# Value pieces and idle matmuls laid out anew between the last head and the first expert, and the second expert's digits computed ahead of its comparisons

## The chip, the cores and the metric

The kernel runs on one core of one Trainium2 chip. The metric is the device time of one execution in microseconds; the comparison uses the median of several executions. A profiled execution gives a trace besides, and its span (first to last instruction) is a little shorter than the time.

## The reference, cut to what matters

```python
def reference(q, k, v, proj, moe_w_gate, moe_w1, moe_w2):
    # attention: 4 batches x 8 heads, 768 positions, 64 wide; a query sees the keys of its own hash bucket
    mask = q_bucket[:, :, :, None] == k_bucket[:, :, None, :]          # buckets: 6 sign bits of q@proj, k@proj
    scores = np.where(mask, scale * q @ k.T, -1e9)
    x = softmax(scores) @ v                                           # -> 3072 tokens x 512
    # mixture of 8 experts, each takes exactly 3072/8 = 384 tokens
    logits = x @ w_gate                                               # 3072 x 8
    for idx in np.argsort(-logits.flatten()):                         # greedy: best (token, expert) pair first
        tok, e = idx // 8, idx % 8
        if assigned[tok] >= 0 or counts[e] >= cap: continue
        assigned[tok] = e; counts[e] += 1
    for e in range(8):
        out[assigned == e] = relu(x[assigned == e] @ w1[e]) @ w2[e]
```

## The kernel before

The 32 heads run one after the other. A head has six key blocks of 128; for each, TensorE makes scores, ScalarE the exponentials, GpSimd or VectorE their low halves, and TensorE multiplies with the values. The last two heads are treated apart: their gate logits come first, so that the assignment of tokens to experts can begin, and their product with the values is cut into **value pieces**, a list `s.rest` of 76 closures (`mains`): per piece three matmuls of 64 columns (L363 to L365), and after each 18 pieces a `close` of three matmuls (L370 or L371) whose result ScalarE scales into X, which SyncE stores. Six are taken up earlier; 70 are left.

The greedy assignment is done in eight phases, one for each expert that fills up (`Moe.phase`). A phase finds a threshold digit by digit: six digits of the logits' bits, and for each a **round** on the path VectorE, TensorE, VectorE, TensorE: VectorE compares the tokens' digits with all values of the digit (L630, `zcmp`), TensorE counts per expert (L640 and 24 matmuls of L641 in the program before, eight columns each), VectorE finds which values reach the expert's room (L743, `zsat`, `zhit`), TensorE sums that into the digit found (L751), VectorE subtracts it (L759, `zd`) and compares the next digit. After the sixth digit come L769 and L770, a chain of small VectorE operations up to the running sum `zcum` (L796), two matmuls (L799, L800), the chain to the one-hot rows `ohp` of the members (L812), 24 matmuls that collect the members' numbers (L815), and `zidx`, with which GpSimd gathers 384 rows of x (L884). Expert weights are fetched as soon as the expert's number is known (L892).

Phase 0 stands between attention and the first expert, and nothing else than value pieces can run in TensorE's pauses. The list `FL` says how many pieces `more(i)` takes at the i-th place: `more(0)` before the last eight counts of the first round, `more(2*l+1)` behind the counts of round l, `more(2*l+2)` behind its L751. Where no pieces are left, **idle matmuls** fill the pauses (`warm`, L682: constants times constants into a tile that nobody reads), so many at each place as `KW` says, of 128 columns unless a third argument says otherwise. Then x is transposed in three chunks (L948), split into halves by ScalarE and VectorE (L949, L950), and the first expert's first layer begins (L965).

Phase 1, for the second expert, runs during the first expert's work: the table `EP` says at which step of it each part of the phase is issued. Its digits 1 to 5 (`digit`, L625 on VectorE) are issued behind its first comparisons and counts. All order on an engine is the order in which the code is written (`manual_schedule`).

Of the kernel before, what the change touches and what calls it, by code (L numbers as in the profile page):

```python
# [14 lines left out]
ALU = mybir.AluOpType  # L15
# [489 lines left out]
E1=[8, 12, 16, 19, 21, 24, 26, 29, 31, 34, 36, 43, 44, 51]  # L505
H1=[2, 0, 2, 2, 0, 3, 0, 2, 2, 0, 1, 0, 0, 0]
ES=[-16, -13, -11, -8, -2, 1, 5, 8, 12, 15, 19, 21, 29, 38]
EP={1: [8, 12, 16, 18, 21, 24, 26, 29, 32, 35, 38, 40, 44, 51], 2: [-5, -3, 1, 4, 8, 11, 15, 18, 22, 25, 29, 32, 39, 47], 3: [-8, -5, -2, 1, 4, 6, 10, 13, 17, 20, 26, 29, 36, 45], 4: [-10, -8, -5, -2, 2, 5, 8, 11, 15, 18, 22, 26, 34, 42]}
WL=[4, 46]
W1=[[], [57, 62, 69, 74], [53, 64, 66, 72], [50, 57, 62, 67], [46, 52, 59, 63], [44, 52, 58, 63]]  # L510
HP={2: [0, 0, 3, 1, 2, 0, 2, 2, 1, 3, 0, 0, 0, 0], 3: [0, 0, 0, 2, 2, 2, 2, 3, 2, 3, 0, 0, 0, 0], 4: [0, 0, 2, 2, 2, 0, 2, 2, 2, 2, 0, 0, 0, 0]}
# [3 lines left out]
OWN=[(2, 0, 0), (3, 0, 0), (4, 0, 0), (5, 0, 0), (3, 1, 3), (4, 1, 3), (5, 1, 3)]  # L515
XS=[56, 56, 57, 57]
XD=[0, 9, 7, 4]
KW=[1,0,5,7,[0,0,6],15,5,1]
SC=[16, 16, 36]
FL=[21, 3, 6, 3, 6, 3, 6, 3, 6, 3, 6, 3, 99]  # L520
XSC=8.0
WSC=64.0
class Moe:
# [72 lines left out]
    def t(s,shape,dt,name,**k): return s.sp.tile(shape,dt,name=name,**k)  # L596
# [79 lines left out]
    def more(s,i):  # L676

        n=FL[i] if i<len(FL) else 0
        while n and s.rest: s.rest.pop(0)(); n-=1
# [4 lines left out]
    def phase(s,ph):  # L684

        nc,NC=s.nc,s.NC; V=nc.vector; T=nc.tensor; G_=nc.gpsimd
# [3 lines left out]
        def ps(): return s.ps0() if first and s.ps0 else s.ps()  # L690
# [3 lines left out]
        if not last:  # L694
            P=s.Z
            D,E,mxu=P["D"],P["E"],P["mxu"]; d=E[:,0]
            CMP=[P["cmp"][l and 1+l%2] for l in range(6)]
            if not first:
                for i,f in enumerate(s.best(P,0,NC)):
                    if ph==1 and i==4: yield  # L700
                    f()
                s.gate=P["OH"][0:1,0,0:1]
                for c0,c1_ in ((0,12),(12,NC)) if ph==1 else ((0,NC),):
                    if ph==1: yield
                    s.compare(CMP[0],0,d,c0,c1_)
                if ph==1: s.gate=CMP[0][0:1,NC//2-1,0,0:1]
            tot=0
            for l,w in enumerate(WID):
                tot+=w; u=2.0**-tot; cmp=CMP[l]
                yield  # L710
                pc=ps()
                if l==0 or first:
                    for c0,c1_ in blocks if first else ((0,NC),):
                        if l: s.compare(cmp,l,d,c0,c1_)
                        if first and l==0 and c1_==NC: s.more(0)
                        s.count(pc,P,cmp,l,c0,c1_)
                    if first:
                        s.more(2*l+1)
                        if not s.rest:
                            if wp is None: wp=s.wps()  # L720
                            s.warm(KW[0],wp)
                        if l==0: s.digit(P,1,slice(0,NC))
                        if l<5:
                            dE=t([128,NC],F32,"dE"); V.scalar_tensor_tensor(dE,D[:,l+1],2.0**-sum(WID[:l+2]),d,op0=ALU.mult,op1=ALU.add)
                    else:
                        for q in range(1,6): s.digit(P,q,slice(0,NC))
                        V.tensor_tensor(E[:,1],D[:,1],s.sc[:,1],op=ALU.mult)
                        for q in range(2,6): nc.scalar.activation(E[:,q],D[:,q],AF.Copy,scale=2.0**-sum(WID[:q+1]))
                        if ph>2:
                            for _ in range(2): s.fill()  # L730
                else:
                    nt=s.count4(pc,P,cmp)

                def carry():
                    g=ps()[:,0:NC]
                    T.matmul(g,s.identb,d,start=True,stop=False)
                    T.matmul(g,s.identb,E[:,l+1],start=False,stop=False)
                    return g
                if not first and 0<l<5: g=carry()
                if l==5: break  # L740
                sat=t([128,8],BF,"sat"); hit=t([128,1],BF,"hit") if l==0 or first else s.hits[l%2]; J=NT[l]
                if l==0 or first:
                    V.tensor_scalar(sat[0:J],pc[0:J,0:8],0.0,0.0,op0=ALU.is_ge,op1=ALU.max,accum_out=hit[0:J])  # L743
                    if first and l<4: s.digit(P,l+2,slice(0,NC))
                else:
                    V.tensor_tensor(sat[0:32],pc[96:128,24:32],nt,op=ALU.is_ge)
                    V.reduce_max(hit[0:32],sat[0:32],axis=AX.X)
                if not first: yield
                if first:
                    pn=ps(); n=pn[:,0:1]  # L750
                    T.matmul(n,s.us[l][0:J],hit[0:J],start=True,stop=True); s.more(2*l+2)  # L751
                    if wp is not None: s.warm(KW[1],wp)
                else:
                    if l==0: g=carry()
                    T.matmul(g,s.nus[l],hit.to_broadcast([128,NC]),start=False,stop=True)
                if l==0 and ph==2:
                    s.fill(); s.fill()
                d2=t([128,NC],BF,"d2",bufs=6)
                if first: V.tensor_tensor(d2,dE,n.to_broadcast([128,NC]),op=ALU.subtract)  # L759
                else:  # L760
                    s.compare(CMP[l+1],l+1,g); V.tensor_copy(d2,g); s.gate=CMP[l+1][0:1,NC//2-1,0,0:1]
                d=d2

            sat=s.satl; s.gate=sat[0:1,0:1]; nn=t([128,1],F32,"nn"); nf=t([128,1],F32,"nf")
            if first: V.tensor_scalar(sat[0:32],pc[0:32,0:8],0.0,None,op0=ALU.is_ge)
            else: V.tensor_tensor(sat[0:32],pc[96:128,24:32],nt,op=ALU.is_ge)
            if not first: yield
            pe=ps()
            T.matmul(pe[:,0:8],s.ones,s.wtb,start=True,stop=False)  # L769
            T.matmul(pe[:,0:8],s.tiny,sat,start=False,stop=True)  # L770
            if first:
                s.more(12)
                if wp is None: wp=s.wps()
                s.warm(KW[2],wp,256)
            V.reduce_max(nn,pe[:,0:8],axis=AX.X)
            wg=t([128,NC],F32,"wg"); e0=t([128,NC],F32,"e0"); A1=t([128,8,NC],BF,"A1"); cc=t([128,8],BF,"cc")
            V.tensor_scalar(nf,nn,ROUND*2.0**-32,ROUND*2.0**-32,op0=ALU.add,op1=ALU.subtract)
            V.scalar_tensor_tensor(wg,d,nn,mxu,op0=ALU.is_gt,op1=ALU.mult)
            V.tensor_scalar(cm,nn,nf,2.0**32,op0=ALU.subtract,op1=ALU.mult)
            if not first: V.tensor_tensor(s.asg,s.asg,wg,op=ALU.add)  # L780
            V.scalar_tensor_tensor(e0,d,nf,mxu,op0=ALU.is_equal,op1=ALU.mult)
            if first: s.widx(ph,cm,t)
            for k,a in enumerate((wg if first else s.asg,e0)): V.tensor_tensor(STb[:,k*NC:k*NC+NC],a,cm.to_broadcast([128,NC]),op=ALU.is_equal)
            if not first: s.widx(ph,cm,t)
        else:
            s8=t([128,8],F32,"s8"); e0=t([128,NC],F32,"e0")
            V.tensor_scalar(c1,s.rem,4.0e4,None,op0=ALU.is_lt)
            V.tensor_tensor(s8,c1,s.wt,op=ALU.mult)
            V.reduce_max(cm,s8,axis=AX.X)
            s.widx(ph,cm,t)  # L790
            V.tensor_scalar(e0,s.asg,cm,None,op0=ALU.is_equal)
            V.tensor_tensor(STb[:,0:NC],e0,s.un,op=ALU.add)
            V.memset(STb[:,NC:],0.0)
# [6 lines left out]
        T.matmul(pp[:,0:2*NC],s.ones,cum,start=False,stop=True)  # L800
        if first: wp=s.psO.tile([128,512],F32,name="po"); s.warm(KW[3],wp,256)
        elif not last:
# [7 lines left out]
        def members(c0,c1):  # L810
            o,i,b=s.paired(md,c0,c1,J,ohp[:,:,0:J],s.iot[:,0:J])
            V.tensor_tensor(o,i,b,op=ALU.is_equal)  # L812
# [29 lines left out]
        if first:  # L842
            pi=ps()
            V.tensor_tensor(Gd,Gt[:,0:6],Gt[:,1:7],op=ALU.subtract)
            V.tensor_tensor(Rr,Gd[:,None].to_broadcast([128,2,6,NC]),s.gp[:,0,:,None,:].to_broadcast([128,2,6,NC]),op=ALU.mult)
            for b,w in zip(((0,8),(8,18),(18,NC)),KW[4]):
                members(*b); collect(*b); s.warm(w,wp,256)
# [18 lines left out]
        if first:  # L866
            left()
            yield
            T.matmul(pp[:,64:72],s.ones,cc,start=True,stop=True)
            s.warm(KW[5],wp,256); s.wp=wp  # L870
        if not last: close(pp[:,64:72])
        yield

# [148 lines left out]
    def run(s):  # L1022
# [8 lines left out]
        for p in range(1,8):  # L1031
            b=NS*(p-1)
            ev=[b+e for e in EP.get(p,ES)]
            hs=H1 if p==1 else HP.get(p,HS)
# [79 lines left out]
```

## Time and profile before

| what | value |
|---|---|
| median of 3 runs (lowest to highest) | 685.28 us (685.08 to 685.69) |
| the profiled execution: time, span | 685.39 us, 683.6 us |
| TensorE busy | 664.8 us (97%) |
| VectorE, ScalarE, GpSimd busy | 501.3, 475.7, 521.7 us |
| mean granted TensorE clock | 0.987 of 2.4 GHz |

A share is the mean over stages of different kinds. What the change touches lies between 370 and 408 us of the span, so it has to be read there.

### The profile page before, as it was taken

How to read it: one execution, taken by the hardware profiler on the slowest of the kernel's cores; microseconds unless marked ns; L12 is line 12 of the kernel's file. 1: busy time of each engine (PE TensorE's matmuls, PEld its weight loads, DVE VectorE, ACT ScalarE, POOL GpSimd, SP SyncE). 2: the span in 40 equal slices, each digit the busy share in tenths (PEclk: the TensorE clock that was granted, in tenths of full speed). 3: DMA queues.
4: the chain of work that ended last, by engine and by line, in shares of the span. 5: the costliest groups of instructions: out<-in, count | busy, mean ns of one | idle time of the engine just before them, and what ended most of it. 6: DMA issues, size and time to landing. Idle time of an engine off the chain costs nothing.

```text
span 683.6 us, 19693 instructions
## 1 busy us (share of the span) xinstructions
PE 664.8 (97%) x8101; PEld 440.0 (64%) x8101; DVE 501.3 (73%) x1127; ACT 475.7 (70%) x906; POOL 521.7 (76%) x466
## 2 busy tenths in 40 slices
PE   8899999999999999999999999999999999999997
PEld 3567676777777777777777775555555555655553
DVE  6778889888877887878878588778778877734120
ACT  7979887888888888877765155765675656666760
POOL 7999998997998989989871156676766665779871
PEclk9999999999999999999999599999999999999999
DMA  8647665526647266460000270717172726272701
GB/s 230 191 121 208 170 175 133 140 76 169 167 100 176 72 144 159 118 150 25 25 2 26 82 237 20 299 39 292 59 280 66 275 91 235 85 269 70 269 32 46
DMA packets 40401, 94.39 MB, mean 138 GB/s; under 512 B 4612, under 2 KB 30584, under 8 KB 38008
## 3 DMA queue, kind: packets, MB, share of 16 engines
q1 hardware_dynamic: 33208, 47.00, 26.2%
q0 software_dynamic: 7104, 46.15, 18.9%
q8 instruction: 63, 1.03, 0.6%
q14 instruction: 26, 0.21, 0.1%
HBM read 60.31 MB, written 12.58 MB: 107 GB/s over the span
## 4 chain that ended last, share of the span: by engine, by line
PE 82%; DVE 6%; ACT 5%; DMA 3%; issue 2%; SPq 1%; another core or an unknown queue 0%; POOLq 0%; ACTq 0%
PE po L992 16%; PE px L980 14%; PE pst L289 8%; PE pst L290 8%; PE pss L265 7%; PE psv L306 4%; PE psv L308 4%; PE psv L307 4%; PE po L980 2%; DVE m L267 2%; PE pss L145 1%; PE pst L400 1%; DMA kb<-kh 1%; DVE lo L294 1%; PE pst L273 1%
## 5 line engine op out<-in xcount | busy, mean ns | idle before, releaser
L294 POOL TENSOR_TENSOR lo<-pt 128x768 f16<-128x768 f32 x138 | 217.1, 1586 | 22.9 <-ACT pt L291 20.0
L291 ACT ACTIVATE pt<-pst 128x384 f32<-128x384 f32 x372 | 175.5, 491 | 52.9 <-PE pst L290 44.1
L267 DVE TENSOR_REDUCE m<-pss 128x1 f16<-128x770 f32 x192 | 181.3, 957 | 35.1 <-PE pss L265 33.8
L289 PE MATMUL pst<-qa,ka 128*128 128x384 f16 x384 | 125.0, 326 | 3.8 <-ACT qa L274 3.0
L290 PE MATMUL pst<-qb,kb 128*128 128x384 f16 x384 | 124.8, 325 | 0.0
L307 PE MATMUL psv<-vl,pt 128*128 128x64 f16 (+1 forms) x1080 | 114.2, 193 | 0.0
L308 PE MATMUL psv<-vh,lo 128*128 128x65 f16 (+1 forms) x1080 | 114.1, 194 | 0.0
L306 PE MATMUL psv<-vh,pt 128*128 128x65 f16 (+1 forms) x1080 | 114.0, 195 | 0.0
L306 PEld LDWEIGHTS <-pt 128*128 128x128 bf16 x1080 | 100.3, 98 | 8.4 <-issue 0.9
L307 PEld LDWEIGHTS <-pt 128*128 128x128 bf16 x1080 | 99.5, 99 | 7.7
L308 PEld LDWEIGHTS <-lo 128*128 128x128 f16 x1080 | 99.6, 97 | 0.0
L919 POOL TENSOR_TENSOR wl<-wf,wh 128x512 f16<-128x512 f32 x74 | 83.7, 1158 | 20.2 <-ACT wf L910 19.7
L265 PE MATMUL pss<-ka,qa 128*128 128x385 f16 x384 | 94.0, 328 | 1.6 <-DMA ka<-bt 0.7
L901 ACT ACTIVATE wh<-wf 128x1024 f16<-128x1024 f32 x64 | 66.9, 1054 | 16.8 <-DMA wf<-in_w_dram,zwidx 16.8
L980 PEld LDWEIGHTS <-wh 128*128 128x128 f16 x480 | 45.3, 97 | 29.8 <-issue 0.7
L992 PEld LDWEIGHTS <-hh 128*128 128x128 f16 x384 | 35.8, 97 | 38.4 <-issue 0.4
L294 DVE TENSOR_TENSOR lo<-pt 128x768 f16<-128x768 f32 (+1 forms) x49 | 58.8, 1205 | 0.7 <-ACT pt L291 0.4
L910 ACT ACTIVATE wf<-wf 128x1024 f32<-128x1024 f32 x55 | 58.0, 1059 | 0.9
L265 PEld LDWEIGHTS <-qa 128*128 128x128 f16 x384 | 37.1, 97 | 27.1 <-issue 1.2
L997 ACT ACTIVATE o<-po 128x512 f32<-128x512 f32 x23 | 13.7, 598 | 56.9 <-PE po L992 50.9
L290 PEld LDWEIGHTS <-kb 128*128 128x128 f16 x384 | 37.4, 97 | 19.2 <-issue 7.2
L884 POOL DMA_INDIRECT xg<-x_dram,zidx x24 | 24.2, 1006 | 30.4 <-DVE zbnd L834 22.5
(383 smaller groups left out, 1453.3 us busy)
## 6 DMA issues: line engine op xcount, KB each, us to landing
vp<-in_vv_dram SPq DMA_DIRECT2D x8, 768.0 KB
x_dram<-X SPq DMA_DIRECT2D x15, 384.0 KB
qp<-in_qT_dram SPq DMA_DIRECT2D x7, 768.0 KB
kp<-in_kT_dram SPq DMA_DIRECT2D x7, 768.0 KB
qa<-qh SPq DMA_DIRECT2D x14, 192.0 KB
qb<-qh SPq DMA_DIRECT2D x14, 192.0 KB
ka<-kh SPq DMA_DIRECT2D x14, 192.0 KB
kb<-kh SPq DMA_DIRECT2D x14, 192.0 KB
```

Source lines behind the costliest of these rows:

```text
L265: T.matmul(ps[:,hf,0:HK],QA[u][:,j,qc*128:qc*128+128],KA[u][:,j,hf*HK:hf*HK+HK],start=True,stop=True)
L267: V.tensor_reduce(M6[h][:,qc:qc+1],ps[:,:,0:HK],axis=AX.XY,op=ALU.max,negate=True)
L289: T.matmul(ps[:,0:384],KA[u][:,j,kr],QA[u][:,j,r],start=True,stop=False)
L290: T.matmul(ps[:,0:384],KB[u][:,j,kr],QB[u][:,j,r],start=False,stop=True)
L291: A.activation(PT[h,kc][0][:,r],ps[:,0:384],AF.Exp,scale=0.125)
L294: eng.tensor_tensor(l[:,r],p[:,r],p.bitcast(BF)[:,1::2][:,r],op=ALU.subtract)
L306: T.matmul(av[:,c,:],ph[:,r],VH[u][:,j,kc,o:],start=(kc==0 and c==0),stop=False,skip_group_check=True)
L307: T.matmul(av[:,c,0:72-o],ph[:,r],VL[u][:,j,kc,o:],start=False,stop=False,skip_group_check=True)
L308: T.matmul(av[:,c,:],l[:,r],VH[u][:,j,kc,o:],start=False,stop=False,skip_group_check=True)
L919: for _ in range(n): s.nc.gpsimd.tensor_tensor(*s.pend.pop(0)[1],op=ALU.subtract)
L980: T.matmul(p[:,0:384],a[:,o:o+128],b[:,d],start=n==0,stop=n==11)
L992: T.matmul(p,a[:,f,c*128:c*128+128],b[:,f*512:f*512+512],start=n==0,stop=n==23)
```

## The change

The number of pieces and idle matmuls at each place is changed. `FL` takes 32 pieces instead of 21 before the last counts of the first round, then 3 and 7 (was 3 and 6), and is used up in the fourth round; what it left over for `more(12)` is gone. `KW` gives the fifth and sixth round idle matmuls of 256 columns (2 behind the counts, 4 behind the sum), then 8 (was 5) behind L770, 16 (was 7) behind L800, 9 (was 6) behind the collecting matmuls, 56 of 128 columns (was 15 of 256) ahead of the transposes, and 6 (was 5) between them. Phase 1's five digits and the scaled second digit move ahead of its first comparisons, and its first part behind those is issued at step 10 instead of 8, where `hand` no longer puts its tiny copy on GpSimd ahead of the weight halves (it does so for steps below 10).

```diff
-EP={1: [8, 12, 16, 18, 21, 24, 26, 29, 32, 35, 38, 40, 44, 51], ...
+EP={1: [10, 12, 16, 18, 21, 24, 26, 29, 32, 35, 38, 40, 44, 51], ...
-KW=[1,0,5,7,[0,0,6],15,5,1]
+KW=[2,4,8,16,[0,0,9],56,6]
-FL=[21, 3, 6, 3, 6, 3, 6, 3, 6, 3, 6, 3, 99]
+FL=[32, 3, 7, 3, 7, 3, 7, 3, 5]
...
+            def digits():
+                for q in range(1,6): s.digit(P,q,slice(0,NC))
+                V.tensor_tensor(E[:,1],D[:,1],s.sc[:,1],op=ALU.mult)
             if not first:
                 for i,f in enumerate(s.best(P,0,NC)):
                     if ph==1 and i==4: yield
                     f()
+                if ph==1: digits()
...
-                            s.warm(KW[0],wp)
+                            s.warm(KW[0],wp,256)
...
-                        for q in range(1,6): s.digit(P,q,slice(0,NC))
-                        V.tensor_tensor(E[:,1],D[:,1],s.sc[:,1],op=ALU.mult)
+                        if ph>1: digits()
...
-                    if wp is not None: s.warm(KW[1],wp)
+                    if wp is not None: s.warm(KW[1],wp,256)
...
             if first:
-                s.more(12)
-                if wp is None: wp=s.wps()
                 s.warm(KW[2],wp,256)
...
-            s.warm(KW[5],wp,256); s.wp=wp
+            s.warm(KW[5],wp); s.wp=wp
```

TensorE, in the fifth round, from the end of its counts on (`zcmp` are the comparisons, `zhit` the values that reached the room, `psv` the value tile): before.

```order
L641 MATMUL pst<-zOH,zcmp_387 32x8
...
L365 MATMUL psv<-vh_223,lo 128x64
L751 LDWEIGHTS us_76
L751 MATMUL pst<-zhit,us_76 128x1
L363 LDWEIGHTS pt
L363 MATMUL psv<-vh_223,pt 128x64
L364 LDWEIGHTS pt
L364 MATMUL psv<-vl_224,pt 128x64
```

The same place of the changed program.

```order
L641 MATMUL pst<-zOH,zcmp_387 32x8
L682 LDWEIGHTS mones
L682 MATMUL pss<-iot,mones 128x256
...
L754 LDWEIGHTS us_76
L754 MATMUL pst<-zhit,us_76 128x1
...
L640 LDWEIGHTS moneh
L640 MATMUL pst<-nrem,moneh 32x8
```

Value pieces stood on both sides of the sum; now two idle matmuls of 256 columns stand ahead of it and four behind it (L751 is L754 in the changed file).

VectorE, where phase 1 goes from its best experts (`zOH`) to its first comparisons (`xl`, `hl` are the first expert's low halves): before.

```order
L616 TENSOR_TENSOR zOH<-zmxu,wt 128x192
L950 SCALAR_TENSOR_TENSOR xl<-psa,xh 128x4x128
L630 TENSOR_TENSOR zcmp_386<-zE,tb_96 128x1536 x2
L969 SCALAR_TENSOR_TENSOR hl<-px,hh 128x4x128
L625 TENSOR_SCALAR zD<-zkey 128x24 x5
L727 TENSOR_TENSOR zE<-zD,sc 128x24
L743 TENSOR_SCALAR zsat,zhit<-psa 128x8
```

And in the changed program.

```order
L616 TENSOR_TENSOR zOH<-zmxu,wt 128x192
L625 TENSOR_SCALAR zD<-zkey 128x24 x5
L700 TENSOR_TENSOR zE<-zD,sc 128x24
L951 SCALAR_TENSOR_TENSOR xl<-psa,xh 128x4x128
L630 TENSOR_TENSOR zcmp_386<-zE,tb_96 128x1536 x2
L970 SCALAR_TENSOR_TENSOR hl<-px,hh 128x4x128
L746 TENSOR_SCALAR zsat,zhit<-psa 128x8
```

The six digit operations went past `xl`, both comparisons and one `hl`, so that nothing of them is left between the counts and `zsat`.

## Rows read from the trace of the kernel before

**Rows 1.** The page: busy time of each engine.
```profile
PE 664.8 (97%) x8101; PEld 440.0 (64%) x8101; DVE 501.3 (73%) x1127; ACT 475.7 (70%) x906; POOL 521.7 (76%) x466
```

**Rows 2.** Windows: length, busy time by engine (instructions), granted clock, DMA share, GB/s.
```profile
365.00:371.90 6.90, 6.90 (x190) 5.89 (x187) 6.15 (x17) 2.85 (x8) 1.10 (x2) 1.00 0.01 2
371.90:375.30 3.40, 2.62 (x80) 2.35 (x77) 2.76 (x18) 0.64 (x3) 0.00 (x0) 0.99 0.02 5
375.30:388.90 13.60, 13.54 (x240) 11.47 (x239) 6.76 (x44) 2.23 (x10) 1.09 (x2) 0.50 0.10 30
388.90:392.40 3.50, 2.52 (x37) 1.86 (x36) 2.77 (x12) 0.01 (x1) 1.92 (x3) 0.99 0.75 228
392.40:395.70 3.30, 3.15 (x16) 1.93 (x15) 2.10 (x8) 1.04 (x1) 2.39 (x4) 0.50 0.74 236
402.00:683.60 281.60, 274.96 (x2111) 157.81 (x2108) 177.88 (x605) 170.38 (x257) 186.43 (x168) 1.00 0.43 153
```

**Rows 3.** Timeline of TensorE in the first round: start, us, instruction [idle before].
```profile
373.25 0.31 PE L641 MATMUL pst<-zOH,zcmp 128*128 128x8 bf16 x6 [0.78 <-DVE zcmp L630]
373.41 0.19 PE L363 MATMUL pss<-vh,pt 128*128 128x64 f16 x1
...
373.50 0.19 PE L363 MATMUL pss<-vh,pt 128*128 128x64 f16 x1
...
373.82 0.16 PE L751 MATMUL pst<-zhit,us 128*128 128x1 bf16 x1
```

**Rows 4.** Timeline of TensorE: the sums of rounds 3 to 5, and L770.
```profile
378.62 0.18 PE L751 MATMUL pst<-zhit,us 32*128 32x1 bf16 x1
...
381.17 0.18 PE L751 MATMUL pst<-zhit,us 32*128 32x1 bf16 x1
...
383.70 0.18 PE L751 MATMUL pst<-zhit,us 32*128 32x1 bf16 x1
...
386.18 0.17 PE L770 MATMUL pst<-satl,tiny 128*128 128x8 bf16 x1
```

**Rows 5.** Timeline of VectorE, 373 to 390 us.
```profile
373.59 0.17 DVE L743 TENSOR_SCALAR_CACHE_REDUCE zsat<-pst 128x8 bf16<-128x8 f32 x1
...
375.38 0.15 DVE L743 TENSOR_SCALAR_CACHE_REDUCE zsat<-pst 32x8 bf16<-32x8 f32 x1 [0.35 <-PE pst L641]
...
384.13 0.69 DVE L630 TENSOR_TENSOR zcmp<-zd,tb 128x256 bf16<-128x256 bf16 x3
...
387.46 0.26 DVE L796 TENSOR_TENSOR_SCAN zcum<-one,zSTb 128x48 bf16<-128x48 f32 x1
...
389.41 1.09 DVE L812 TENSOR_TENSOR zcmp<-zmd,iot 128x512 bf16<-128x512 bf16 x3
```

**Rows 6.** Timeline of TensorE, 387 to 397 us, idle matmuls and what they surround.
```profile
387.90 0.21 PE L800 MATMUL psa<-zcum,mones 128*128 128x48 bf16 x1
387.94 1.39 PE L682 MATMUL po<-iot,mones 128*128 128x256 bf16 x7
389.88 1.09 PE L815 MATMUL psa<-zRr,zcmp 128*64 128x12 bf16 x24 [0.55 <-issue]
...
392.17 0.17 PE L869 MATMUL psa<-zcc,mones 128*128 128x8 bf16 x1 [0.43 <-DVE zA L826]
392.19 3.27 PE L682 MATMUL po<-iot,mones 128*128 128x256 bf16 x15
...
396.15 0.71 PE L682 MATMUL po<-iot,mones 128*128 128x256 bf16 x5
```

**Rows 7.** Timeline of TensorE's weight loads: the first transposes.
```profile
395.62 0.46 PEld L948 LDWEIGHTS px<-identf,xg 128*128 128x128 f32 x4 [0.63 <-DMA xg<-x_dram,zidx]
```

**Rows 8.** First expert: the digits' line (ns min/median/max); timelines of GpSimd and TensorE.
```profile
L625 DVE TENSOR_SCALAR zD<-zkey x6: 165/167/1198, 401.4 to 407.2; 128x24 int32<-128x24 int32 x6
...
404.85 2.27 POOL L919 TENSOR_TENSOR wl<-wf,wh 128x512 f16<-128x512 f32 x2
...
401.50 0.22 PE L965 MATMUL px<-xh,wh 128*128 128x128 f16 x1 [1.10 <-issue]
```

More of the change, by code (lines that the diff above doesn't have):

```diff
@@ L507 @@
 ES=[-16, -13, -11, -8, -2, 1, 5, 8, 12, 15, 19, 21, 29, 38]
-EP={1: [8, 12, 16, 18, 21, 24, 26, 29, 32, 35, 38, 40, 44, 51], 2: [-5, -3, 1, 4, 8, 11, 15, 18, 22, 25, 29, 32, 39, 47], 3: [-8, -5, -2, 1, 4, 6, 10, 13, 17, 20, 26, 29, 36, 45], 4: [-10, -8, -5, -2, 2, 5, 8, 11, 15, 18, 22, 26, 34, 42]}
+EP={1: [10, 12, 16, 18, 21, 24, 26, 29, 32, 35, 38, 40, 44, 51], 2: [-5, -3, 1, 4, 8, 11, 15, 18, 22, 25, 29, 32, 39, 47], 3: [-8, -5, -2, 1, 4, 6, 10, 13, 17, 20, 26, 29, 36, 45], 4: [-10, -8, -5, -2, 2, 5, 8, 11, 15, 18, 22, 26, 34, 42]}
 WL=[4, 46]
```

## The prediction, written before the changed kernel ran

> **What bounds the kernel now.** The page first: TensorE is busy for 97% of the span, the others for 70 to 76% [rows 1]. Such a mean hides where time can be won, so I cut the span into windows and read the granted clock beside the busy time. From 402 us to the end TensorE is busy for 274.96 of 281.60 us at full clock [rows 2]: whatever brings the first expert forward goes through to the end nearly whole. Ahead of it lies the one place where the clock falls. Up to 371.9 it is granted 1.00, which is 2.4 GHz; from 375.3 to 388.9 it is 0.50, 1.2 GHz, and once more from 392.4 to 395.7 [rows 2]. Before the first fall TensorE was busy for only 2.62 of 3.40 us, before the second for 2.52 of 3.50; before the rises it ran without a break, at the end on idle matmuls of 256 columns. But dense is not enough: in the 13.6 us at half clock it is busy for 13.54 us all the same [rows 2]. So I read the fall as the price of the pause and of what surrounds it.
>
> The pause itself is in the timeline: 0.78 us ahead of the last counts of the first round, for the comparisons of VectorE [rows 3]. From there on the rounds are a chain over two engines, and TensorE's share of it doubles in length. At half clock a round takes 2.54 us (378.62 to 381.17 to 383.70) and the last stretch to L770 2.48 [rows 4].
>
> **The change part by part, and what each costs.**
>
> *32 pieces instead of 21.* A piece takes 0.09 us at full clock (373.41 to 373.50) [rows 3], so eleven take 1.0 us and, with a close among them, perhaps 1.1, where 0.78 us are free. The last counts start some 0.1 to 0.3 us later. I take the sum of the first round at 373.97 instead of 373.82. The pause is gone, and I expect no fall at 375.3.
>
> *Four rounds at full clock.* The only round of before that ran at full clock in nearly all of its length gives the size: from L751 at 373.82 to the next `zsat` at 375.38 are 1.56 us, and from a `zsat` to its sum 0.23 (373.59 to 373.82) [rows 3, 5]. That is 1.79; the seventh piece adds 0.09, so 1.88. A close is among the pieces in two of the four and counts as about a piece. 373.97 + 4 x 1.88 = 381.49, against 383.70 [rows 4]: 2.2 us won. VectorE does not hold them at 2.54, since its three comparisons take no more than 0.69 us of it [rows 5]. The bounds: 1.79, if the seventh piece hides, and 2.3, if a close costs a piece more and each matmul its drain.
>
> *The last stretch.* Four idle matmuls stand where six pieces stood. At half clock 15 of them take 3.27 us, 0.22 each, and five at full clock 0.71 with the last one's drain [rows 6]; I take 0.11, half of 0.22. Four end after 0.44 us, before the comparisons do: those of before start 0.43 us after the sum (384.13 after 383.70) and take 0.69 [rows 4, 5]. Eight counts, `zsat` and the two behind it add about 0.6. I take 1.75 instead of 2.48: L770's successor at 383.24, 2.9 us earlier.
>
> *From L770 to the transposes nothing gets shorter.* VectorE's chain to `zcum` ends at 387.72, 1.54 us behind L770, and L800 follows at 387.90 [rows 4 to 6]. Eight idle matmuls (0.9 us) fit beneath it. From L800 to the collecting L815 are 1.98 us, in which VectorE makes the one-hot rows (389.41) [rows 5, 6]; 16 idle matmuls take 1.8 and fit, with 0.2 to spare. From the collection to L869 TensorE waits for VectorE for 0.43 us at the end, and six idle matmuls ran there [rows 6]; three more cost 0.33 and fit. The cover in each case is VectorE's chain.
>
> *56 of 128 columns instead of 15 of 256.* At full clock half of 0.11, so 56 x 0.055 = 3.1 us, where 3.27 stood at mostly half clock [rows 6]. The cover is the gather: the first transposes' weights came in at 395.62 for the DMA of x [rows 7]. Its issue hangs on `zidx` and moves forward with the chain. So the transposes move by the same 2.9 us, to about 392.7. One more idle matmul after each of the first two chunks costs up to 0.22; the next chunk's gather covers it if that is late, and I count 0.05.
>
> *Digits ahead of comparisons.* Six digit operations take 165 to 167 ns, but one took 1198 while GpSimd's L919 ran from 404.85 [rows 8]. Moved, they run where GpSimd only issues DMAs, and `zsat` is up to 1 us earlier. TensorE has first-layer work meanwhile, so little of that reaches the end. Against it, the comparisons come later by the six operations and run into L919, which no longer waits for them. Between a gain of 0.3 and a loss of 1.2 (below) I take nothing, since TensorE's counts also come two steps later.
>
> [...]
>
> *132 more rows in TensorE's program.* It stood 1.10 us in front of a matmul of the first expert, for nothing that the profile names [rows 8]. The rows behind come at other places of the program. Such a stop may vanish (a gain of 1.1), move into an idle stretch, or come twice (a loss of 1.1); I take none.
>
> [...]
>
> **The sum.** 2.9 won up to the transposes, less 0.05, nothing for the rest: 685.39 - 2.9 = 682.5. The profiled execution lies 0.1 above the median of 685.28, so 682.4 stands against that. Own range of this case, from the bounds above (1.1 and 0.3 won, 1.2 lost): 681.1 to 683.7.
>
> **Rivals.**
>
> *The clock falls later all the same (chance 0.22).* For it: at half clock TensorE stayed there through rounds that were without pauses [rows 2], and the new rounds hold the same narrow counts. Against it: it kept its clock for the 6.90 us before, with 190 short matmuls and no pause [rows 2]. If it falls in the third round, the two rounds before have won about 0.9 us (2 x 1.88 from 373.97 is 377.73, against 378.62 [rows 4]); each later one costs 2.54 plus 0.2 for the seventh piece, so 0.4 of it goes; and 16 idle matmuls at half clock take 3.5 us against the gap of 1.98, 1.5 too long, of which a rise in the middle of them, as at 388.9, leaves some 0.4. 685.39 - 0.9 + 0.4 + 0.4 = 685.3. That is also the case that the change doesn't do what it says.
>
> *Idle matmuls overrun (slower, 0.10).* The place: the 16 behind L800 and the 56 ahead of the transposes. They are real work for an engine that must finish them before the chain's next matmul. At half clock the 16 take 3.5 against 1.98 us and the 56 take 56 x 0.11 = 6.2 against 3.3 [rows 6], so 1.5 and 2.9 too long; a rise halfway, as at 388.9 and 395.7 [rows 2], halves both. With nothing won in the rounds (the clock falls as before), the result is 685.39 + 0.5 x 4.4 = 687.6. It decides from about half of these stretches at 1.2 GHz on.
>
> *The lock or the stop takes a part back (0.14).* One of phase 1's two comparisons of 128x1536 starts after L919 and is blocked for one instruction, 1.14 us (2.27 for two) [rows 8], as the digit of 1198 ns was; the counts two steps later wait for it, or the unnamed stop of 1.10 comes once more. 685.39 - 2.9 + 1.15 = 683.6. No comparison was blocked before, because GpSimd waited for it.
>
> **How the numbers follow.** Main case 0.52 at 682.5, its part taken back 0.14 at 683.6, the late fall 0.22 at 685.3, the overrun 0.10 at 687.6, and 0.02 for something else. A measurement here tells about 0.2%, 1.37 us, from no change; that is 683.9 and 686.65. Faster by more: the first two, 0.66. Within: the late fall and a little of the overrun, 0.24. Slower: 0.10. The range leaves out the overrun and the edge of the main case: 681.3 to 685.6. Against the median of before the likeliest is 682.4.
>
> **What would show it right or wrong.** Right: granted clock 1.00 from 372 to 392 us, sums of the rounds 1.8 to 1.95 us apart, no pause of 0.78 us ahead of the eight counts, L815 preceded by a short wait for VectorE, the first transposes at 392 to 393, one digit line without a 1198. Wrong: a window at 0.50 anywhere between 376 and 392; L815 or the transposes directly behind the last idle matmul with no wait in between (the overrun); a comparison of 128x1536 that lasts 2 us (the lock); TensorE standing 1 us in the first expert at two places (the stop). If the span shrinks by 3 us and the clock was low, I would be right by accident.

## The result, and the profile after

| | before | after |
|---|---|---|
| median, us | 685.18 (681.23 to 688.39, 18 executions) | 688.94 (687.81 to 693.97, 18 executions) |
| ratio after/before | | 1.0063, 95% interval 1.0045 to 1.0081 |
| profiled execution, us (span) | 685.39 (683.6) | 689.41 (687.6) |
| mean granted clock of it | 0.987 | 0.998 |

The change makes the kernel 0.6% slower. I had forecast 0.4% faster, and the range ended at 685.6.

The windows of after, in the stretches of [rows 2] (length, busy time by engine, granted clock, DMA share, GB/s):
```profile
371.90:375.30 3.40, 3.40 (x108) 3.14 (x105) 2.52 (x16) 1.11 (x5) 0.00 (x0) 1.00 0.08 24
375.30:388.90 13.60, 13.13 (x260) 10.90 (x259) 9.53 (x55) 1.55 (x8) 2.76 (x4) 1.00 0.26 76
388.90:392.40 3.50, 3.32 (x57) 3.13 (x56) 2.30 (x9) 1.01 (x1) 2.60 (x3) 1.00 0.77 247
392.40:395.70 3.30, 1.49 (x11) 1.08 (x12) 0.00 (x0) 0.00 (x0) 2.68 (x3) 1.00 0.74 207
395.70:402.00 6.30, 4.97 (x44) 4.26 (x44) 2.42 (x4) 3.30 (x5) 1.08 (x2) 0.73 0.97 337
402.00:687.60 285.60, 276.45 (x2119) 158.03 (x2115) 179.89 (x615) 169.42 (x256) 187.10 (x167) 1.00 0.42 148
```
Up to 392.4 all is as forecast: the pause is gone (3.40 of 3.40 us busy) and the clock stays at 1.00, where 0.50 stood (16 idle matmuls of 256 columns take 1.91 us behind L801; at 0.50, 15 of them took 3.27 [rows 6]). Then come two rows that I had not expected. From 392.4 to 395.7 TensorE is busy for 1.49 of 3.30 us, and VectorE and ScalarE for nothing at all. From 395.7 to 402 the granted clock falls after all, to a mean of 0.73.

The timeline of TensorE shows the place (start, us, instruction, [idle before]; L754 is L751 of before, L773 L770, L801 L800, L816 L815, L870 L869, L949 L948):
```profile
377.57 0.17 PE L754 MATMUL pst<-zhit,us 32*128 32x1 bf16 x1
...
379.49 0.17 PE L754 MATMUL pst<-zhit,us 32*128 32x1 bf16 x1
...
383.07 0.17 PE L773 MATMUL pst<-satl,tiny 128*128 128x8 bf16 x1
...
384.65 0.18 PE L801 MATMUL psa<-zcum,mones 128*128 128x48 bf16 x1
384.68 1.91 PE L682 MATMUL po<-iot,mones 128*128 128x256 bf16 x16
386.61 1.10 PE L816 MATMUL psa<-zRr,zcmp 128*64 128x12 bf16 x24
...
388.90 0.17 PE L870 MATMUL psa<-zcc,mones 128*128 128x8 bf16 x1
388.92 3.30 PE L682 MATMUL po<-iot,mones 128*128 128x128 bf16 x56
393.16 0.66 PE L949 MATMUL px<-identf,xg 128*128 128x128 f32 x4 [0.94 <-DMA xg<-x_dram,zidx]
394.14 0.71 PE L682 MATMUL po<-iot,mones 128*128 128x256 bf16 x5 [0.33 <-issue]
395.57 0.27 PE L682 MATMUL po<-iot,mones 128*128 128x256 bf16 x1 [0.72 <-issue]
...
397.03 0.60 PE L682 MATMUL po<-iot,mones 128*128 128x256 bf16 x4 [0.75 <-issue]
...
398.50 0.40 PE L682 MATMUL po<-iot,mones 128*128 128x256 bf16 x1 [0.42 <-issue]
398.69 1.06 PE L949 MATMUL psa<-identf,xg 128*128 128x128 f32 x4
```
The sums come every 1.92 us; L773 stands at 383.07, 3.1 us ahead of [rows 4]; L870 is 3.27 ahead of [rows 6]. The first transposes start at 393.16, only 2.46 ahead of [rows 7], after a wait for the gather. Behind them TensorE stands five times, for 0.15 to 0.75 us, in front of idle matmuls, which wait for no data. And ScalarE, which has only to make `xh`, the high halves, of what those first transposes wrote, comes 4.9 us after their end. The timelines of ScalarE, before (0.78 us behind the start of the transposes) and after (5.54 us):
```profile
396.40 0.60 ACT L949 ACTIVATE xh<-px 128x512 f16<-128x512 f32 x1 [2.96 <-DVE nrem L839]
```
```profile
398.70 0.60 ACT L950 ACTIVATE xh<-px 128x512 f16<-128x512 f32 x1 [8.79 <-remote]
```
"Remote" means that the profile knows no local instruction that would explain the wait.

The second loss is of another kind. VectorE before, then VectorE and GpSimd after:
```profile
401.35 0.17 DVE L625 TENSOR_SCALAR zD<-zkey 128x24 int32<-128x24 int32 x1
...
401.57 0.17 DVE L615 TENSOR_TENSOR zE<-zD,sc 128x24 bf16<-128x24 int32 x1
```
```profile
403.52 1.01 DVE L625 TENSOR_SCALAR zD<-zkey 128x24 int32<-128x24 int32 x1
...
404.56 1.11 DVE L615 TENSOR_TENSOR zE<-zD,sc 128x24 bf16<-128x24 int32 x1
...
405.87 0.49 DVE L625 TENSOR_SCALAR zD<-zkey 128x24 int32<-128x24 int32 x5
```
```profile
403.33 2.30 POOL L920 TENSOR_TENSOR wl<-wf,wh 128x512 f16<-128x512 f32 x2 [6.24 <-ACT wf L911]
```
Two tiny operations of VectorE, the first digit and its scaling, take 1.01 and 1.11 us while GpSimd's casts (L920, L919 of before) run; they took 0.17 before, where those casts came later. Neither is one of the operations that were moved: the five moved digits take 0.49 us here, and nothing blocks them.

So the bookkeeping of the two profiled executions, from four marks: the first transposes, the first matmul of layer 1 (L965, now L966), GpSimd's next load of a weight matrix, and the end. The transposes are 2.46 us earlier. L966 is at 399.54, where 398.64 stood: 3.36 lost by the **late xh**. The load is issued at 426.18 instead of 424.05: another 1.23, with the **blocked VectorE** in it. Up to the end 1.9 more go in the experts 2 to 4. -2.46 + 3.36 + 1.23 + 1.9 = 4.0, which is the difference of the spans.

### The profile page after: what moved, and what is told of

Read it like the earlier page. It is cut to its first block, busy times and chain, and to the rows that moved or that the text cites. A ratio compares the mean times of both kernels' runs of the same rounds, so it can differ in the third digit from the quotient of the medians.

```text
span 687.6 us, 19823 instructions
## 1 busy us (share of the span) xinstructions
PE 665.8 (97%) x8167; PEld 441.2 (64%) x8167; DVE 501.7 (73%) x1127; ACT 475.1 (69%) x906; POOL 522.4 (76%) x465
## 4 chain that ended last, share of the span: by engine, by line
PE 71%; DMA 9%; DVE 7%; ACT 5%; issue 3%; SPq 2%; another core or an unknown queue 1%; POOL 1%; POOLq 0%; ACTq 0%; DVEq 0%
PE po L993 13%; PE px L981 12%; PE pst L289 8%; PE pst L290 7%; PE pss L265 7%; PE psv L306 4%; PE psv L308 4%; PE psv L307 4%; DMA wf<-in_w_dram,zwidx 4%; DVE m L267 2%; ACT wh L902 2%; ACT wf L911 1%; DMA kb<-kh 1%; PE pst L400 1%
## 5 line engine op out<-in xcount | busy, mean ns | idle before, releaser
L920 POOL TENSOR_TENSOR wl<-wf,wh 128x512 f16<-128x512 f32 x74 | 84.8, 1172 | 31.0 <-ACT wf L911 30.5
```

Source lines behind the costliest of these rows:

```text
L920: for _ in range(n): s.nc.gpsimd.tensor_tensor(*s.pend.pop(0)[1],op=ALU.subtract)
```

## The experiments

Theory A: the many instructions that TensorE issues just ahead of the transposes are what makes xh late. Theory B: the digits in front of the comparisons, with the second expert's first place at 10 instead of 8, cost the time by way of VectorE and GpSimd. Theory C: the stretch is bound by when its DMAs land. Kernels of one group ran on one chip, beside the kernel before; a time of one group is compared with others of that group only. "xh n us behind" counts from the start of the first transposes.

**First group: each half by itself** (before 683.59).

*28 idle matmuls of 256 columns for 56 of 128:*
```diff
-KW=[2,4,8,16,[0,0,9],56,6]
+KW=[2,4,8,16,[0,0,9],28,6]
-            s.warm(KW[5],wp); s.wp=wp
+            s.warm(KW[5],wp,256); s.wp=wp
```


> The changed kernel with 28 idle matmuls of 256 columns ahead of the transposes instead of 56 of 128: the same columns and so the same TensorE time (3.1 us at full clock), half the instructions. If it is the number of instructions issued just ahead of the DMA-heavy stretch that starves TensorE and holds ScalarE's first xh back (theory A), the stop-and-go after the first transposes shrinks, xh starts 2 us or more earlier than 398.70, and the time falls by 2 to 4 us, to about 685 to 687. If the digits in front of the comparisons cost the time (theory B), or the stretch is bound by when its DMAs land (theory C), it stays within 1 us of the changed kernel, at 688 to 690.

Measured 683.62, ratio 0.9999 (0.9979 to 1.0019).

*The layout alone:*
```diff
-EP={1: [10, 12, 16, 18, 21, 24, 26, 29, 32, 35, 38, 40, 44, 51], 2: [-5, -3, 1, 4, 8, 11, 15, 18, 22, 25, 29, 32, 39, 47], 3: [-8, -5, -2, 1, 4, 6, 10, 13, 17, 20, 26, 29, 36, 45], 4: [-10, -8, -5, -2, 2, 5, 8, 11, 15, 18, 22, 26, 34, 42]}
+EP={1: [8, 12, 16, 18, 21, 24, 26, 29, 32, 35, 38, 40, 44, 51], 2: [-5, -3, 1, 4, 8, 11, 15, 18, 22, 25, 29, 32, 39, 47], 3: [-8, -5, -2, 1, 4, 6, 10, 13, 17, 20, 26, 29, 36, 45], 4: [-10, -8, -5, -2, 2, 5, 8, 11, 15, 18, 22, 26, 34, 42]}
-                if ph==1: digits()
-                        if ph>1: digits()
+                        digits()
```


> The changed kernel with the digits back behind the comparisons and the second expert's first place back at 8, so the layout of pieces and idle matmuls alone. Theory B (comparisons of 128x1536 delayed by the digits and caught by GpSimd's casts): the time falls to 686 or below, since the waits of TensorE for the comparisons at 407 to 409 (0.5 to 1.2 us) and what hangs on them go. Theories A and C: the loss ahead of it (2.1 us at the first L981 at least) stays, xh still starts at about 398.7, time 687 to 689.

Measured 683.35, ratio 1.0001 (0.9986 to 1.0015).

*The digits alone,* the reverse of that edit, made in the kernel before (the `EP` line with 10 and the definition of `digits()` go with it and are not shown):
```diff
+                if ph==1: digits()
-                        for q in range(1,6): s.digit(P,q,slice(0,NC))
-                        V.tensor_tensor(E[:,1],D[:,1],s.sc[:,1],op=ALU.mult)
+                        if ph>1: digits()
```


> The kernel before with the digits in front of the comparisons and the second expert's first place at 10, the layout untouched. Theory B: slower by 1 to 3 us, 686.5 to 688.5, with comparisons that start 0.5 to 1 us later and a matmul that waits for them. Theories A and C: within 0.7 us of before.

Measured 683.76, ratio 1.0008 (0.9993 to 1.0023). The 1 to 3 us that theory B wants do not come, although the two comparisons do last longer, 3.22 us instead of 1.82, beside GpSimd's casts.

*15 of 256:* the first diff with 15 for 28.

> The changed kernel with 15 idle matmuls of 256 columns ahead of the transposes, as many as before, which at full clock take 1.65 us instead of 3.1. TensorE then pauses some 1.5 to 2 us for the gather. Theory A: 30 instead of 112 instructions there, no starving, xh within 1 us of the transposes, time 684 to 686 unless the clock falls in the pause, which costs up to 1 us. Theory C: transposes and xh as late as in the changed kernel, 688 to 690. If the clock after such a pause is the price that the 56 were to save, the stretch from 392.4 shows 0.50 for longer than the changed kernel does.

Measured 684.65, ratio 1.0015 (0.9997 to 1.0033). In all of the group xh follows its transposes by 0.74 to 0.76 us: nothing could be told of the late xh here. What can be told is that the layout alone, which holds the clock, wins nothing against the median of before. It even lies 1.2 us above the ten executions of before in this group whose mean clock is 0.995 or more (median 682.1).

**Second group: the changed kernel as control, and the digits' edit in two** (before 683.50).

> The changed kernel once more, unaltered, beside its three variants on one chip. If its loss belongs to the kernel and not to the chip of the first comparison, it is slower than before by 0.4 to 0.8%, 686.5 to 689, with TensorE's stop-and-go between 394 and 399 and the first xh 4 us behind its transposes. If the loss belongs to that chip or to that hour, it lies within 0.2% of before, like the two variants already run.

The changed kernel: 684.95, ratio 1.0019 (0.9996 to 1.0041). No late xh in this profile either; the loss is smaller, and it sits at 400 to 408. The median lies in a gap: six of its twelve executions took 682.29 to 683.51 us and six 686.38 to 687.90, and the profile (686.49) is one of the second six.

*Place 8, digits in front:* the `EP` line of above alone.

> The changed kernel with the second expert's first place back at 8, digits still in front. If the stop-and-go hangs on what TensorE's queue holds behind the transposes (its order differs from the layout alone only there), this shows which half of the edit does it: with the place at 8 the stall goes, 683 to 685; if the order of VectorE's digits does it, it stays at 686.5 to 689.

Measured 682.88, ratio 0.9995 (0.9974 to 1.0016).

*Place 10, digits behind:* the other lines alone.

> The changed kernel with the digits behind the comparisons again and the first place left at 10. If VectorE's order and GpSimd's casts that start without waiting cost the time (theory B), 683 to 685; if the place of the counts in TensorE's order does it, 686.5 to 689 with the stall between 394 and 399.

Measured 685.35, ratio 1.0033 (1.0012 to 1.0054).

*28 of 256, place 8, digits behind.*

> Both edits that took the loss away singly, together: 28 idle matmuls of 256 columns ahead of the transposes, digits behind the comparisons, first place 8. If the loss was one stall that either of them removes, nothing more is won: within 1 us of each of them, so 0.0 to 0.2% from before. If they remove two different losses it is faster than either by 1 to 2 us, 681.5 to 682.5 beside a before of 683.6.

Measured 683.41, ratio 1.0000 (0.9984 to 1.0016).

At place 10, digits in front or behind are not told apart (684.95 against 685.35). Between the places lie 2.1 us of median (684.95 against 682.88), but the changed kernel's lower six executions lie only 0.3 above it (683.18) and the upper six 3.8 (686.65). What sets these halves apart is not known; the profile of the upper half shows what differs from place 8. VectorE, then GpSimd, in the changed kernel:
```profile
400.10 2.43 DVE L625 TENSOR_SCALAR zD<-zkey 128x24 int32<-128x24 int32 x5
...
403.15 2.78 DVE L630 TENSOR_TENSOR zcmp<-zE,tb 128x1536 bf16<-128x1536 bf16 x2
```
```profile
400.21 2.30 POOL L920 TENSOR_TENSOR wl<-wf,wh 128x512 f16<-128x512 f32 x2 [2.46 <-ACT wf L911]
403.78 3.16 POOL L920 TENSOR_TENSOR wl<-wf,wh 128x512 f16<-128x512 f32 x2 [1.28 <-ACT wf L911]
```
The same engines with place 8:
```profile
399.61 0.50 DVE L625 TENSOR_SCALAR zD<-zkey 128x24 int32<-128x24 int32 x5
...
400.71 1.82 DVE L630 TENSOR_TENSOR zcmp<-zE,tb 128x1536 bf16<-128x1536 bf16 x2
```
```profile
402.60 0.18 POOL L919 CAST ztick<-zcmp 1x1 f32<-1x1 bf16 x1 [5.34 <-DVE zcmp L630]
402.76 4.50 POOL L920 TENSOR_TENSOR wl<-wf,wh 128x512 f16<-128x512 f32 x4
```
With place 8 GpSimd makes a copy of one element first, which waits for the comparisons; its casts start when VectorE is through. With place 10 the program has no such copy (`s.hand(n,s.now<10)`: it is issued only below 10), the casts start at 400.21, and digits and comparisons together take 5.21 us instead of 2.32: 2.43 beside 0.50 and 2.78 beside 1.82. That GpSimd's casts hold VectorE's operations up while they run is my reading of such pairs, called the lock below; by what way one engine holds the other up no run shows.

**Third group: the copy put back, and two single executions** (before 683.02).

*Place 10 with the copy:*
```diff
-            next(ch[p],None); s.hand(n,s.now<10)
+            next(ch[p],None); s.hand(n,s.now<11)
```


> The changed kernel, place 10 and digits in front, with GpSimd's one-element copy that waits for the second expert's last comparison put back ahead of its first casts (place 10 had dropped it). Lock theory (the earlier casts block VectorE's digits and comparisons, 2.43 instead of 0.50 and 2.78 instead of 1.82 us): digits 0.5, comparisons 1.8 us, TensorE's waits before 407 fall to 0.5 us or less, time 682.5 to 683.5, like the variant with place 8 (682.88). Place theory (the counts two places later leave too little time to the next step): the wait stays though nothing is locked, 684.5 to 686.

Measured 686.90, ratio 1.0060 (1.0037 to 1.0082). Nothing is blocked any more, as the lock theory has it (timeline of VectorE):
```profile
403.65 0.50 DVE L625 TENSOR_SCALAR zD<-zkey 128x24 int32<-128x24 int32 x5
...
404.75 1.82 DVE L630 TENSOR_TENSOR zcmp<-zE,tb 128x1536 bf16<-128x1536 bf16 x2
```
and yet both numbers that were expected are missed, because here the late xh is there: 398.21, 5.12 us behind the start of the transposes. From L966 to the next weight load, a stretch behind the late xh, are 25.10 us, against 26.64, 28.00 and 26.83 in the three profiles of the changed kernel and 24.48 to 25.78 in the three with place 8, digits in front and 56 idle matmuls. So in these profiles the missing copy, not the place, is what costs. It does not cost always: the three kernels without it in the first group have 25.13 to 25.67 us in this stretch. When the blocking reaches the end, and when not, is open.

*Place 8 with 28 of 256:*

> Place 8, so with GpSimd's wait, digits in front, and 28 idle matmuls of 256 columns instead of 56 of 128 ahead of the transposes. If half the instructions there take a stall away that this kernel still has in a part of its runs, 681.5 to 682.5, and faster than before by 0.2%; if the number of instructions does nothing once the casts wait, 682.5 to 683.5 as with place 8 alone.

Measured 684.23, ratio 1.0017 (0.9995 to 1.0039). xh is late here too (396.74, 3.71 behind), though TensorE never stands in front of an idle matmul: the last transposes start at 395.27, and it waits for xh afterwards.

*The changed kernel, and before, one execution each:*

> The changed kernel once more, one look. If the stop-and-go of 394 to 399 belongs to this kernel in a part of its executions, it may be seen again; if it does not show, TensorE's waits in 401 to 408 should, with digits or comparisons that take 1 us longer beside GpSimd's casts. 683 to 689 either way.

688.54; xh 4.64 us behind, and the first digit and its scaling blocked (1.01 and 1.12 us) as in the first profile.

> The kernel before once more, one look. Of 70 executions beside the experiments about a third show a mean clock of 0.995 or more and lie near 681.8, the others near 684.5. In a profile of the first kind the first round's pause is there and the clock holds all the same, and L770 stands near 383.5 instead of 386.2; in one of the second kind it repeats the known profile.

683.06, xh 0.74 us behind. The pause of the first round is there (0.79 us up to 372.17, so in part ahead of the first window), and the clock falls two rounds later than in [rows 2]: the first sums are 2.04, 1.83, 2.40 and 2.54 us apart here (372.75, 374.79, 376.62, 379.02, 381.56), and 2.26 and then three times some 2.54 there. The windows of this execution:
```profile
371.90:375.30 3.40, 3.13 (x83) 2.78 (x84) 2.25 (x16) 0.54 (x3) 0.00 (x0) 1.00 0.00 0
375.30:388.90 13.60, 13.19 (x248) 10.93 (x245) 8.03 (x48) 1.68 (x8) 2.22 (x3) 0.62 0.21 61
```
This is neither of the two kinds that I had expected, but one between them.

**Fourth group: what the late xh hangs on** (before 684.04).

*The first expert's second weight matrix loaded only behind the last xh:*
```diff
+        s.xsplit0()
+        s.nc.gpsimd.tensor_copy(s.z([1,1],F32,"tick"),s.W[0,'x'][0][0:1,0,383:384])
         s.wload(0,1,2)
-        s.xsplit0()
```


> The changed kernel with the load of the first expert's second weight matrix (2 transfers, 2 MB) issued only when the last xh is written, instead of right behind the gather. If DMA traffic beside the transposes is what holds xh and TensorE back, the first xh comes within 1 us of its transposes and TensorE does not stop between 394 and 399; what the casts cost by blocking VectorE stays or moves, since the later load also makes the second matrix's casts later: 683 to 686. If the late xh has nothing to do with this traffic, it is seen again (on a chip that shows it at all) and the time stays at 685 to 689.

Measured 688.77, ratio 1.0069 (1.0045 to 1.0094); xh 2.92 us behind. VectorE blocked for longer than ever (one digit 2.85 us).

> Place 8 (the casts wait for the comparisons) and the later load together. If both costs are real and add up, the best so far: 681 to 682.5, 0.1 to 0.3% faster than before. If the later load makes the second matrix late for layer 2, TensorE waits there and it is 684 or more.

Measured 685.52, ratio 1.0028 (1.0007 to 1.0049); xh 2.12 behind. It was to be the best so far if both costs were real and added up, and it is not. The place, and with it the copy, makes 3.25 us between these two.

> The changed kernel with place 8 alone, once more, as the control for the other three on this chip. Lock theory: 682.5 to 684, faster than the changed kernel was on any chip (684.95 to 688.94); on a chip with the late xh it keeps that loss and lies at 684 to 686.

Measured 687.79, ratio 1.0060 (1.0041 to 1.0080); xh 5.27 behind. So the same kernel that gave 682.88 in the second group, with xh 0.74 behind, is 4.9 us slower here, above both expectations: the late xh comes and goes. It is not the chip alone, since the second and the fifth group ran on the same one and this same kernel has 0.74 in the one and 5.77 in the other. With the second matrix's load deferred the delay is smaller (2.12 against 5.27, 685.52 against 687.79), and does not go. By what way is not shown: from 392.4 to 395.7, where xh becomes late, the DMA share of that version is not lower (0.88, against 0.67); the two loads that it defers are issued at 395.11 and 396.35 in this one.

> Place 8 with 15 idle matmuls of 256 columns ahead of the transposes. If the number of idle matmuls ahead of the transposes matters for the late xh, it is better than the control by 1 us or more on a chip that shows it; otherwise within 0.7 us of the control, with TensorE waiting about 2 us for the gather and the clock as the profile shows it (1.00 in the same variant with place 10).

Measured 683.38, ratio 0.9990 (0.9974 to 1.0005); xh 0.74 behind, on the chip where the control has 5.27. In its pause of 2.65 us for the gather the clock did fall, to a mean of 0.86 and 0.80 in the two windows from 392.4 to 402.

**Fifth group: instructions or time** (before 684.12). Same columns, same place, same time of TensorE:
```diff
-            s.warm(KW[5],wp); s.wp=wp
+            i2=s.iot.rearrange("p j q -> p (j q)")[:,None,:].to_broadcast([128,2,256])
+            for _ in range(KW[5]): s.nc.tensor.matmul(wp.rearrange("p (a b) -> p a b",a=2),s.ones,i2,start=True,stop=True)
+            s.wp=wp
```
with `KW[5]` 14, and place 8.

> Place 8, and ahead of the transposes 14 idle matmuls of 512 columns: TensorE's time as with 56 of 128 (some 3.1 us), 28 instructions instead of 112. If the number of instructions makes xh late, it comes within 1 us of the transposes and the time is 682.5 to 684 on any chip. If TensorE's running right up to the transposes does it, xh is late wherever it is late in the control.

Measured 683.29, ratio 0.9986 (0.9970 to 1.0002).

> Place 8 with the 56 idle matmuls of 128 columns, the control on this chip: 682.5 to 684 where the chip shows no late xh, 686 to 688 with xh 3 us or more behind its transposes where it does. Only in the second case does the pair say what the late xh hangs on.

Measured 687.77, ratio 1.0048 (1.0030 to 1.0066): 4.5 us apart, and no execution of the one reaches the other (682.03 to 685.87, 686.74 to 688.81). TensorE, then ScalarE, with 14 of 512:
```profile
389.28 3.18 PE L872 MATMUL po<-iot,mones 128*128 128x512 bf16 x14
392.92 0.65 PE L951 MATMUL px<-identf,xg 128*128 128x128 f32 x4 [0.46 <-issue]
393.41 0.82 PE L682 MATMUL po<-iot,mones 128*128 128x256 bf16 x6
394.07 0.60 PE L951 MATMUL px<-identf,xg 128*128 128x128 f32 x4
...
398.72 0.33 PE L968 MATMUL px<-xh,wh 128*128 128x128 f16 x3 [1.10 <-issue]
```
```profile
393.66 0.60 ACT L952 ACTIVATE xh<-px 128x512 f16<-128x512 f32 x1 [3.77 <-issue]
...
395.91 0.60 ACT L952 ACTIVATE xh<-px 128x512 f16<-128x512 f32 x1 [0.70 <-PE psa L951]
398.80 0.60 ACT L952 ACTIVATE xh<-psa 128x512 f16<-128x512 f32 x1 [2.29 <-remote]
```
and with 56 of 128:
```profile
388.13 3.34 PE L682 MATMUL po<-iot,mones 128*128 128x128 bf16 x56
392.14 0.66 PE L949 MATMUL px<-identf,xg 128*128 128x128 f32 x4 [0.67 <-DMA xg<-x_dram,zidx]
...
393.40 0.49 PE L682 MATMUL po<-iot,mones 128*128 128x256 bf16 x3 [0.23 <-issue]
393.72 0.38 PE L949 MATMUL px<-identf,xg 128*128 128x128 f32 x2
394.84 0.43 PE L949 MATMUL px<-identf,xg 128*128 128x128 f32 x2 [0.74 <-issue]
```
```profile
397.91 0.60 ACT L950 ACTIVATE xh<-px 128x512 f16<-128x512 f32 x1 [8.77 <-remote]
...
399.35 0.59 ACT L950 ACTIVATE xh<-px 128x512 f16<-128x512 f32 x1
399.83 0.60 ACT L950 ACTIVATE xh<-psa 128x512 f16<-128x512 f32 x1
```
Both fill TensorE for 3.2 to 3.3 us right up to the gather. A matmul and its weight load are two instructions (the page of before counts 8101 of each [rows 1]), so one has 28 of them and the other 112. With 28 the first xh is prompt, and standing and late xh come later and smaller: 1.10 us, as in before [rows 8], and a third xh 3.6 us behind its transposes (3.4 in before). In the first two groups xh was never late, not in the four profiles with 112 instructions either. Over all other profiles: with 28 or 30 instructions ahead of the transposes (the two of before among them) the first xh was late in none of four, with 56 in the one there is, with 112 in all seven. The pair changes the number and the width of the matmuls together. That it is the number rests on two versions of one width, 256 columns, from two groups: late with 56 instructions (3.71 us), prompt with 30.

## Why the prediction was wrong

**Pieces, rounds, last stretch: right.** L773 was forecast at some 383.2 and stands at 383.07; rounds of 1.88 us are 1.92; the clock holds up to 392. For the 2.4 and 1.2 GHz that stand beside the shares 1.00 and 0.50, the runs have rates alone, an estimate from idle matmuls of 256 columns: 0.109 us each at 1.00 (16 in 1.91 us, five in 0.71), some 2.35 columns per ns, and 0.22 at 0.50 (15 in 3.27 [rows 6]), some 1.17. The chain to the transposes was nearly right: the gather, which hangs on `zidx`, is issued 3.27 us earlier (388.34 against 391.61), but the transposes come only 2.46 earlier, not 2.9, since its first chunk takes 0.8 us longer. What the clock is worth is seen in before itself: of its 130 executions in the five groups, 62 have a mean clock of at most 0.989 and a median of 684.9, and 45 of at least 0.995, with 682.1. These 2.8 us fit the 2.9 of the sum.

**But I took one profiled execution for the kernel.** It is of the first kind; in a third of the executions there was next to nothing of the clock's price to win. Against the medians of before in the five groups (683.0 to 684.1) 1 to 2 us were to be had, not 2.9.

**The step that failed: "*132 more rows in TensorE's program* ... I take none", bounded at 1.1.** Most of these rows are the 56 idle matmuls for 15, which I costed by their time alone, under the cover of the gather. The cover was there: TensorE still waits 0.94 us for the DMA behind them. The price is in how many and how narrow they are: 4.5 us in the fifth group, 3.4 up to L966 in the first profile. The row that should have warned me is the 1.10 of [rows 8]. It told of a stop of TensorE, in the same DMA-heavy stretch, that I could not price, and I let it weigh nothing. What came was larger and of another form: not a stop of TensorE alone, but a first xh up to 5.77 us behind the start of its transposes.

**The digits: "Between a gain of 0.3 and a loss of 1.2 (below) I take nothing".** The mechanism stood in the text, that GpSimd "no longer waits"; the size was wrong. "Moved, they run where GpSimd only issues DMAs" does not hold either: in the second group's profile of the changed kernel they run beside the casts. Both digits and comparisons can be caught, not one instruction. The price between versions without and with the copy is 2.1 and 3.25 us in two pairs, 1.2 in the first profile, and nothing to be seen in the first group. The gain of 0.3 is not told from nothing.

**"Whatever brings the first expert forward goes through to the end nearly whole": not quite.** Between the loads of the second and third experts' weights, 33.4 us apart in both profiles of before, the changed layout needs 0.6 to 1.0 more in all profiles but one, with a prompt xh or a late one (421.01 to 455.42 with 14 of 512, against 421.58 to 454.97 in the second profile of before). The second expert's transposes wait there twice for a chunk of the gather, some 0.33 us each with 14 of 512; why the gather lands later is open.

**The rivals.** "The lock or the stop takes a part back" named the lock and a stop of TensorE, one at a time and at 1.15 us; it did not name a late xh. That the digit of 1198 ns beside 167 [rows 8] was blocked by GpSimd's cast, and for one instruction of it, was my estimate: the runs show the lengths beside casts, 1.01 and 1.11 us in the first profile and 2.85 with the second matrix loaded late, for operations that take 0.17 without, and not what makes them so. Lock and late xh came together and at about 4.6 (3.36 and 1.23). The late fall did not happen in the rounds; the clock fell only behind 395.7, after TensorE had stood. Of the overrun one sign is there, L816 directly behind the last idle matmul, but at 1.96 us from L801, where it was 1.98, so it cost nothing. Theory C falls as far as the gather goes: in the fifth group the transposes are earlier in the kernel that ends later.

**What stays open.** Shown is that 56 narrow idle matmuls in place of 14 wide ones bring the late xh where it comes at all, and that it does not come in every hour. That it is by their number is the best reading, not shown apart from their width; that DMA traffic adds to it rests on one pair of profiles; by what way is unknown. It is not TensorE's standing alone (in the version with place 8 and 28 of 256 it never stood, and xh was 3.7 us late). Nor is a fetch of instructions seen at the stop: in the fifth group's control the queue q8, whose packets the profile calls instruction, moves 0.02 MB between 389.00 and 389.25 and again between 403.25 and 403.50, and between these only q14, of the same kind, 0.01 MB between 390 and 391.

**The best version** is place 8 with 14 of 512: 4.5 us faster than its twin with 56 of 128. Against before its ratio is 0.9986, with an interval that ends at 1.0002: probably 0.1% faster, not shown.

## What to carry to other kernels

Work that only fills a pause can have a price besides its time: here, ahead of a stretch full of DMAs (a share of 0.97 from 395.7 to 402 in the first profile), 14 wide matmuls were the safer filling, 683.29 us against 687.77 with 56 narrow ones that keep TensorE busy about as long (3.18 and 3.34 us). When a moved table entry drops a wait, put a price on the wait: here a 10 for an 8 dropped the one that kept GpSimd's casts behind VectorE's digits and comparisons (2.32 us with it, 5.21 without), and I knew it and took nothing. And look at the scatter of the kernel before: if some of its executions already run without the cost that is to go, only the rest can win.

## What the runs showed of the hardware that was not expected

ScalarE's first read of the transposes came 2.1 to 5.8 us behind their start (0.74 to 0.78 otherwise) in eight profiles, all with 56 or 112 instructions of idle matmuls just ahead. The same program shows it on one occasion and not on another, on one chip (0.74 and 5.77 us, 682.88 and 687.77). The DMA share does not tell the two apart: from 392.4 to 395.7 it is 0.67 to 0.88 in the eight, and 0.71 to 0.80 in four profiles with a prompt xh (the changed kernel and place 8 of the second group, 14 of 512, place 8 with 15 of 256).

A pause of 0.78 us was followed by the fall of the granted clock to 0.50 within the next round in the first profile; one of 0.79 us, with the same work around it, two rounds later than that in another; and in a third of the executions (45 of 130) the mean clock, 0.995 or more, says that there was hardly a fall.
